# The output's zeroes are sent after W_out's loads instead of among them, and the planner's priorities are set anew

## The chip, the core and the metric

One NeuronCore of a Trainium2 chip runs the whole program. The metric is the device time of one execution in microseconds, median of several runs. Engines are named as the profile names them: PE (TensorE matmul; PEld its weight loads), DVE (VectorE), ACT (ScalarE), POOL (GpSimd), SP (SyncE, which here only issues DMAs).

## What is computed

Three stages follow each other. (1) A Nystrom attention for 4 batches of 8 heads, 576 tokens, 64 wide, with 32 landmarks per head. (2) A mixture of 8 experts, top-1: each token goes to one expert and is multiplied by its gate. (3) A dense MLP with a leaky ReLU whose slope is given per hidden unit.

```python
A = sm(q, k_lm); Bm = sm(q_lm, k_lm); C = sm(q_lm, k)
Z = Bm.T / (norm1(Bm) * norminf(Bm) + 1e-06)
for _ in range(6):
    Z = 2 * Z - Z @ Bm @ Z
x = A @ Z @ C @ v
logits = x @ w_gate
out[i] = gate_w[i] * (relu(x[i] @ w1[e]) @ w2[e])
h = x @ w_in
g = maximum(h, 0) + alpha * minimum(h, 0)
return g @ w_out
```

## The kernel before

Attention is done per batch b and per group g of four heads: `attend_c` makes the landmark-to-token side (C, Bm and Y = C v), `attend_a` the token-to-landmark side (A). `attention_post` iterates Z and makes the routing logits: once for batch 0 alone (stream "post0"), once for the other three (stream "post"). The rest works on one pair of batch and expert at a time. The expert of the first token of batch 0 is read as soon as batch 0's logits are there (`first_expert` writes `e0i`; `weights` reads it on SP and loads that expert's W1 and W2), and this first pair is done in straight code while the other batches are still in attention. The other pairs are in a list, and a hardware loop (`For_i` in `run`) does one per pass; in these inputs there are two passes. One pair is: landmark rows (`landmark_rows`, W1 folded with the attention's small factors into the fp16 pair MW), `moe_h` (hidden tile of the expert, MW times xT), `moe_y` (times W2), transposes, `moe2_h` (times W_in), `moe2_out` (times W_out) and `rows_out`, which scatters the finished rows to the output by an indirect DMA on POOL. Every product is made of three fp16 passes from a high and a low part, so each weight is loaded as float64 words, narrowed to float32 on DVE (three instructions per pair of row blocks, `narrow`), squared and summed on ACT for a scale, and split into two fp16 parts on ACT and DVE (`split`).

W_out's sixteen row blocks come in eight pairs, by way of two stages of SBUF (`st64`, names st_4 to st_11 in the order): the load of a pair waits until the pair two before it has been narrowed. The narrowed pairs lie in room that is free by then (tiles W, MW and xT), and are split to WO at the end. The rows of the output that no pair scatters must be zero: `clear` sends the tile `zero` to the whole output by 18 DMAs of 256 KB, and a scatter may start only when they have landed.

No engine's order is written by hand. Each piece of work is a generator (a stream) that yields one instruction at a time, and `Plan.run` picks, over all streams, which instruction is emitted next: it has a cost for each instruction (`Lane.cost`), takes the stream that could start first, and lets a stream of lower rank go before it if that one could start within `patience + EAGER * (difference of rank)` (`by`). Ranks are numbers in the table `RANKS` (per b and g) and at the streams. `until` holds a stream back in the plan alone; the waits on the chip come from the data. `keep_warm` puts fill matmuls (`fill`, L1728, zero times ones) in front of a PE instruction for which the plan expects PE to wait. The chosen order is fixed when the program is built, each engine runs its own list in order, and SP's list is the order of the DMAs.

Of the kernel before, what the change touches and what calls it, by code (L numbers as in the profile page):

```python
# [18 lines left out]
LM = 32  # L19
TG = 18  # L20
# [184 lines left out]
class Plan:  # L205
# [4 lines left out]
    PHASE = 600  # L210
    EAGER = -62.784

# [172 lines left out]
class Kernel:  # L385
# [41 lines left out]
    def constants(self):  # L427
# [28 lines left out]
        self.have.add("constants")  # L456
        self.streams["constants"].own = -64.376
        def iota(name, n, pattern, base=0, mult=0, parts=P, dt=F32):
# [71 lines left out]
    def loads(self):  # L530

        for b in range(self.B):
            for g in range(2):
                heads = slice(4 * g, 4 * g + 4)
                self.streams["loads"].own = RANKS[b][g] + -54.682
                for nm, src in (("k", self.k), ("q", self.q)):
                    self.raw[nm, b, g] = t = yield Get(self.S["qk"])
                    yield self.dq.dma_start(t, src[b, heads].rearrange("h (p j) d -> (h p) j d", j=TG))
                    self.have.add((nm, b, g))
                if (b, g) == (0, 0):  # L540
                    self.streams["values"] = yield Fork(self.values(), -58.523)

    def values(self):

        for b in range(self.B):
            for g in range(2):
                heads = slice(4 * g, 4 * g + 4)
                if (b, g) != (0, 0):
                    self.streams["values"].own = RANKS[b][g] + -58.501
                self.raw["v", b, g] = t = yield Get(self.S["v"])  # L550
                src = self.v[b, heads]
                yield self.dq.dma_start(t[:, :, :4].rearrange("p h t d -> p h (t d)"), src[:, : 4 * P].rearrange("h (p t) d -> p h (t d)", t=4))
                yield self.dq.dma_start(t[:64, :, 4], src[:, 4 * P :].rearrange("h p d -> p h d"))
                self.have.add(("v", b, g))
                if (b, g) == (0, 0):
                    self.tc.prologue_barrier()

    def sums(self):
# [3 lines left out]
        for b in range(self.B):  # L562
            for g in range(2):
                self.streams["sums"].own = RANKS[b][g] + -55.120
                i = 2 * b + g
# [23 lines left out]
    def turn(self):  # L589
# [8 lines left out]
        for b in range(self.B):  # L598
            for g in range(2):
                self.streams["turn"].own = RANKS[b][g] + -60.592  # L600
                dst = yield Get(self.S["qkT"])
# [70 lines left out]
    def attend_c(self, b, g):  # L672
# [61 lines left out]
    def attend_a(self, b, g):  # L734
# [31 lines left out]
        self.have.add(("P", b, g))  # L766
        self.streams["store", b, g] = yield Fork(self.store(b, g, parts), -53.748)

# [7 lines left out]
    def attention_post(self, bs):  # L776
# [79 lines left out]
        if b == 0:  # L856
            self.streams["post0"].own = -64.244
        big = yield Get(self.big)
# [52 lines left out]
        for n, bb in enumerate(bs):  # L911
# [18 lines left out]
            if bb == 0:  # L930
                yield from self.first_expert(L[0:1, 0, 0, :])
                self.streams["post0"].own = 69.663
            yield Fork(self.used(bb, AT))
        self.have.add(("x", bs[-1]))
        if b:
            yield self.until(("routed", 0))
            self.streams["post"].own = -67.282
        yield from self.route(bs, L)
# [36 lines left out]
    def route(self, bs, L):  # L975
# [82 lines left out]
        if b == 0:  # L1058

            i0 = self.ar.tile([P, 5], F32, tag="r_i0", name="r_i0")  # L1060
            yield dve.scalar_tensor_tensor(i0, code[:, 0], self.e0c, row[:, 0], op0=ALU.is_equal, op1=ALU.mult)
            yield dve.tensor_scalar(self.idx0, i0, float(self.NT), None, op0=ALU.add)
            self.have.add("idx0")
            self.streams["post0"].own = -56.297
        table = self.table[:, b * E : (b + nb) * E].rearrange("p q t -> p (q t)")
# [137 lines left out]
    def landmark_rows(self, MT, slots, late=0.0):  # L1203
# [25 lines left out]
        yield ended(kids)  # L1229
        scale = yield Fork(self.scale_of("w1", 4), -61.376)  # L1230
        yield ended([scale])
# [37 lines left out]
    def early(self):  # L1269
# [11 lines left out]

        self.streams["early_loads"] = yield Fork(loads(), 65.505)
        kids = []
# [41 lines left out]
    def convert(self, name, n, amax=None, low="d", load=None, first=0):  # L1325
# [8 lines left out]
        yield ended(kids)  # L1334
        scale = yield Fork(self.scale_of(name, n // 2, amax), -63.884)
        yield ended([scale])
# [11 lines left out]
    def weight2(self, name, src, amax, low, first=0):  # L1348
# [9 lines left out]
        if name == "wi":  # L1358
            self.streams["wi_loads"] = yield Fork(self.fetch(name, src, range(first, 16, 2), arrived), -71.763)
        else:  # L1360
            self.streams["wo_loads"] = yield Fork(self.fetch(name, src, range(first, 16, 2), arrived), -65.336)
        yield from self.convert(name, 16, amax, low, lambda i: self.narrowed(name, i, arrived), first)
# [191 lines left out]

    def moe2_out(self, ts):

# [51 lines left out]
    def pre(self):  # L1608

        yield self.until(("P", 0, 0), ("P", 0, 1), *([("used", self.n_early - 4)] if self.n_early else ["early"]))  # L1610
        self.streams["first"].own = -64.283
# [4 lines left out]
        self.streams["first"].own = -52.364  # L1616
# [3 lines left out]
        self.streams["first"].own = -61.768  # L1620
        yield from self.moe2_h(True)
        self.have.add("h2")

    def weights(self):
# [3 lines left out]
        yield from self.load_expert(bass.ds(e0, 1), ["w1"])  # L1628
        self.streams["rows"] = yield Fork(self.landmark_rows(self.MT[:, 0:2], [self.big] * 2), -64.966)
        yield self.until("early")  # L1630
        self.streams["weights"].own = -54.431
        yield from self.load_expert(bass.ds(e0, 1), ["w2"])
        self.streams["weights"].own = 64.801
        yield from self.convert("w2", 8, low='d')
# [32 lines left out]
    def clear(self):  # L1667

        yield self.until('y')
        for t in range(self.NT // P):  # L1670
# [48 lines left out]
    def run(self):  # L1719
# [15 lines left out]
        with tc.manual_schedule(engines={ET.PE, ET.DVE, ET.Activation, ET.Pool, ET.SP}):  # L1735
# [24 lines left out]
            for _ in range(10):  # L1760
# [7 lines left out]
                "first": Stream(self.pre(), -58.952),  # L1768
                "weights": Stream(self.weights(), -54.630),
                "rooms": Stream(self.rooms(), -55.921),  # L1770
                "post": Stream(self.attention_post(list(range(1, self.B))), -55.955),
                "early": Stream(self.early(), 70.830),
                "wi": Stream(self.weight_in(), 70.305),
                "wo": Stream(self.weight_out(), 72.429),
                "clear": Stream(self.clear(), 73.613),
                "experts": Stream(self.experts(), 70.932),
                "out": Stream(self.first_out(), -64.384),
                "next": Stream(self.first_next(), -69.294),
                "next_w1": Stream(self.next_w1_late(), -69.303),
                "next_w2": Stream(self.next_w2('d'), -60.504),  # L1780
            }
            for b in range(self.B):
                for g in range(2):
                    self.streams["c", b, g] = Stream(self.attend_c(b, g), RANKS[b][g] + -68.234)
                    self.streams["a", b, g] = Stream(self.attend_a(b, g), RANKS[b][g] + 58.649)
            for lane, ns in ((self.dq, 600), (self.dve, 1200), (self.act, 2000), (self.gp, 1800), (self.pe, 700 + 213 * 10)):
# [40 lines left out]
```

## Time and profile before

| | |
|---|---|
| median of 3 runs | 532.61 us (532.55 to 534.73) |
| the profiled execution | 531.96 us, of which 527.9 us are the span from the first to the last instruction |
| PE busy | 505.1 us, 96% of the span |
| DVE busy | 297.6 us, 56% |
| ACT busy | 260.1 us, 49% |
| POOL busy | 88.2 us, 17% |
| DMA | 64.47 MB, mean 122 GB/s |
| granted TensorE clock | 0.998 |

In time: attention and the first pair's expert run to about 151 us, `moe2_h` of the first pair to 205 us, its `moe2_out` to 257 us, and the two passes of the loop fill the rest. PE's 96% count a matmul from its issue to its modelled end, so a wait of a matmul inside a group can be hidden in it, and the 173 fill matmuls are counted as work too. The figures between the first instruction and 260 us are the ones that the change can move: the loop's code is the same but for a few neighbours exchanged.

### The profile page before, as it was taken

What the parts mean: (1) busy time and instruction counts of PE and PEld (TensorE: products, weight loads), DVE (VectorE), ACT (ScalarE), POOL (GpSimd) and SP (SyncE); (2) the same over time, 40 slices, a digit from 0 to 9 for tenths busy, and PEclk for the clock granted to TensorE, in tenths of its full rate; (3) what the DMA queues carried; (4) which work ended last, traced back from release to release, by engine and by line L of the source; (5) the groups of instructions that cost most, each with busy time, mean ns of one, the idle gap of its engine ahead of it and who ended that gap; (6) DMA issues with size and microseconds to landing.
All of it is one profiled execution on the core that took longest, in us unless ns stands there. A gap on an engine that the chain in (4) does not pass through costs nothing.

```text
span 527.9 us, 12141 instructions
## 1 busy us (share of the span) xinstructions
PE 505.1 (96%) x4808; PEld 333.1 (63%) x4808; DVE 297.6 (56%) x712; ACT 260.1 (49%) x579; POOL 88.2 (17%) x139
## 2 busy tenths in 40 slices
PE   9899988999999699999999999999999999999996
PEld 6777765877477476445655876744475577684444
DVE  6878899869999798306242566820023256584000
ACT  4665646684678469426332458810023245883000
POOL 4888200000114433002100000000010000000101
PEclk9999999999999999999999999999999999999999
DMA  8997548734798722801002390000000229000100
GB/s 298 309 331 259 172 143 271 261 107 137 214 230 240 268 87 84 280 1 60 32 1 50 78 327 7 1 8 33 20 30 0 50 45 339 23 0 0 40 20 31
DMA packets 50682, 64.47 MB, mean 122 GB/s; under 512 B 20320, under 2 KB 34032, under 8 KB 50640
## 3 DMA queue, kind: packets, MB, share of 16 engines
q1 hardware_dynamic: 49536, 60.34, 37.1%
q0 software_dynamic: 1104, 3.54, 1.8%
q8 instruction: 30, 0.49, 0.4%
q14 instruction: 12, 0.10, 0.1%
HBM read 49.50 MB, written 10.62 MB: 114 GB/s over the span
## 4 chain that ended last, share of the span: by engine, by line
PE 74%; DVE 10%; issue 6%; DMA 3%; POOL 2%; ACT 1%; POOLq 0%; SPq 0%; ACTq 0%; DVEq 0%
PE mm L81 70%; PE big L81 2%; DMA out<-st,idxc 2%; PE mm L1728 2%; DVE MW L81 1%; DMA st<-in_moe_w_out 1%; DVE W L81 1%; DVE WIa L81 1%; DVE mm L81 1%; DVE T L81 1%; DVE hgA L81 1%; POOL WIa L81 1%; DVE g L81 1%; POOL hgB L81 1%; DVE mx L81 0%
## 5 line engine op out<-in xcount | busy, mean ns | idle before, releaser
L81 PEld LDWEIGHTS <-hgA 128*128 128x128 f16 (+1 forms) x864 | 70.5, 102 | 69.1 <-issue 5.8
L81 PEld LDWEIGHTS <-WIa 128*128 128x128 f16 x864 | 84.2, 98 | 31.3 <-issue 9.8
L81 PE MATMUL mm<-WO,hgA 128*128 128x512 f16 (+1 forms) x432 | 72.8, 344 | 0.0
L81 PE MATMUL mm<-WO,hgB 128*128 128x512 f16 (+1 forms) x432 | 72.8, 344 | 0.0
L81 PE MATMUL mm<-W,hgA 128*128 128x512 f16 (+1 forms) x432 | 72.7, 344 | 0.1
L81 PE MATMUL mm<-yB,WIa 128*128 128x320 f16 x432 | 61.5, 299 | 4.9 <-DVE g L81 3.7
L81 POOL DMA_INDIRECT out<-st,idxc x12 | 12.3, 1027 | 287.9 <-ACT st L81 282.8
L81 ACT ACTIVATE st<-mm,fac 128x512 f32<-128x512 f32 (+1 forms) x15 | 9.7, 644 | 99.3 <-PE mm L81 99.2
L81 PEld LDWEIGHTS <-hgB 128*128 128x128 f16 (+1 forms) x432 | 35.3, 102 | 36.1 <-issue 3.3
L81 PE MATMUL mm<-yA,WIa 128*128 128x256 f16 x432 | 50.6, 273 | 2.3 <-DVE g L81 1.7
L81 ACT ACTIVATE g<-mm 128x256 f32<-128x256 f32 (+1 forms) x96 | 39.2, 412 | 22.4 <-PE mm L81 13.8
L81 DVE SCALAR_TENSOR_TENSOR mm<-g,oma,mm 128x256 f32<-128x256 f32 (+1 forms) x80 | 41.0, 517 | 9.1 <-ACT g L81 8.5
L81 PE MATMUL mm<-xT,MW 128*128 128x320 f16 (+1 forms) x288 | 36.9, 286 | 2.4 <-ACT st L81 1.8
L81 PEld LDWEIGHTS <-MW 128*128 128x128 f16 x288 | 27.8, 98 | 9.9 <-issue 1.7
L81 PEld LDWEIGHTS <-WIb 128*128 128x128 f16 x288 | 28.2, 99 | 7.3 <-issue 0.4
L81 ACT ACTIVATE junk<-mm 128x512 bf16<-128x512 f32 (+1 forms) x27 | 15.5, 573 | 34.3 <-PE mm L81 34.0
L81 ACT COPY qkT<-mm 128x512 f32<-128x512 f32 (+1 forms) x48 | 22.5, 525 | 18.7 <-PE mm L81 18.7
L81 DVE COPY idxc<-idxn 128x5 int32<-128x5 int32 x2 | 0.3, 173 | 54.9 <-issue 43.9
L81 ACT ACTIVATE hgA<-mm 128x256 f16<-128x256 f32 (+1 forms) x48 | 19.3, 410 | 15.0 <-PE mm L81 14.6
L81 DVE TENSOR_TENSOR hgA<-mm,hgA 128x256 f16<-128x256 f32 (+1 forms) x40 | 18.2, 455 | 14.1 <-ACT hgA L81 13.9
L81 DVE SCALAR_TENSOR_TENSOR hgA<-mm,hgA 128x256 f16<-128x256 f32 (+1 forms) x48 | 20.7, 454 | 9.3 <-ACT hgA L81 9.3
L81 ACT ACTIVATE junk<-W 128x1024 bf16<-128x1024 f32 x21 | 22.2, 1056 | 7.5 <-DMA W<-in_moe_w 7.0
(286 smaller groups left out, 751.2 us busy)
## 6 DMA issues: line engine op xcount, KB each, us to landing
W<-in_moe_w SPq DMA_DIRECT2D x8, 1024.0 KB, 7.9
st<-in_moe_w_out SPq DMA_DIRECT2D x16, 512.0 KB, 5.1
hgA<-in_moe_w_in SPq DMA_DIRECT2D x10, 512.0 KB, 6.5
qk<-in_k SPq DMA_DIRECT2D x8, 576.0 KB, 5.6
qk<-in_q SPq DMA_DIRECT2D x8, 576.0 KB, 7.6
out<-zero SPq DMA_DIRECT2D x18, 256.0 KB, 4.7
v<-in_v SPq DMA_DIRECT2D x8, 512.0 KB, 5.1
W<-in_moe_w SPq DMA_DIRECT2D x8, 512.0 KB, 5.1
```

The source lines that it names most:

```text
L81: r = getattr(self.lane.engine, name)(*a, **k)
L1728: nc.tensor.matmul(o[:, :256], self.ones16, self.zero.bitcast(F16), start=True, stop=True)
```

## The change

`clear` waits in the plan for W_out to be loaded and narrowed too; `first_out` does not wait for `clear` any more, but the first pair's scatters do. All ranks, the table `RANKS` and `EAGER` have new numbers, so the planner's order of everything up to the loop is a new one. One activation of `attend_c` has lost a cost that was set by hand (the plan's own formula stands for it). No instruction of the computation is added or taken away; the plan issues 174 fill matmuls where it issued 173.

```diff
-RANKS = [[-74.375, -56.288], [-49.431, -65.912], [71.374, -74.373], [72.660, -62.802]]
+RANKS = [[-190.251, -162.415], [-189.669, -24.286], [-21.570, 79.087], [95.553, -68.442]]
...
-    EAGER = -62.784
+    EAGER = -23.848
...
-        yield act.activation(EC.rearrange("p (m j w) -> p m j w", m=LM, w=2), turned, AF.Exp, bias=nm2[:, 0:1], scale=0.125 / TG, accum_out=sums[:, 0:1]).takes(1.0)
+        yield act.activation(EC.rearrange("p (m j w) -> p m j w", m=LM, w=2), turned, AF.Exp, bias=nm2[:, 0:1], scale=0.125 / TG, accum_out=sums[:, 0:1])
...
-    def moe2_out(self, ts):
+    def moe2_out(self, ts, first=False):
...
-                    yield Fork(self.rows_out(x, t))
+                    yield Fork(self.rows_out(x, t, first))
...
-    def rows_out(self, ps, t):
+    def rows_out(self, ps, t, first):
...
         yield Put(ps)
+        if first:
+            yield self.until("clear")
         yield self.gp.indirect_dma_start(
...
     def clear(self):
 
-        yield self.until('y')
+        yield self.until("y", ("wo", "float32"))
         for t in range(self.NT // P):
...
     def first_out(self):
 
-        yield self.until("h2", "clear", ("wo", 0))
+        yield self.until("h2", ("wo", 0))
...
-            yield from self.moe2_out(ts)
+            yield from self.moe2_out(ts, True)
...
-                "constants": Stream(self.constants(), 56.007),
-                "post0": Stream(self.attention_post([0]), -64.166),
+                "constants": Stream(self.constants(), -68.342),
+                "post0": Stream(self.attention_post([0]), -168.986),
...
-                "clear": Stream(self.clear(), 73.613),
+                "clear": Stream(self.clear(), -178.670),
```

The first place is SP's list around the second half of W_out's loads (st_8 to st_11 are the pairs that begin with row blocks 8, 10, 12 and 14; x_lst is the list of pairs). Before:

```order
L81 DMA_TRANSPOSE yB<-y_120 128x4x64 x2
L81 DMA out<-zero 512x1x128 x3
L81 DMA st_8_2750<-in_moe_w_out 128x1024 x2
L81 DMA out<-zero 512x1x128 x9
L81 DMA st_9_2868<-in_moe_w_out 128x1024 x2
L81 DMA out<-zero 512x1x128
L1792 TENSOR_LOAD x_lst
L1792 ISA x2
L81 DMA st_10_2965<-in_moe_w_out 128x1024 x2
L81 DMA st_11_3051<-in_moe_w_out 128x1024 x2
L81 TENSOR_LOAD x_lst
```

And now, on SP at the same place:

```order
L81 DMA_TRANSPOSE yB<-y_120 128x4x64 x2
L81 DMA st_8_2745<-in_moe_w_out 128x1024 x2
L81 DMA st_9_2854<-in_moe_w_out 128x1024 x2
L1794 TENSOR_LOAD x_lst
L1794 ISA x2
L81 DMA st_10_2948<-in_moe_w_out 128x1024 x2
L81 DMA st_11_3034<-in_moe_w_out 128x1024 x2
L81 DMA out<-zero 512x1x128 x18
L81 TENSOR_LOAD x_lst
```

The five zeroes further up have left too: all 18 now stand between the last load of W_out and the reading of the list, behind which the next expert's loads come.

The second place is DVE's list from batch 0's logits (L) to the number of its expert (e0i); WIa<-hgA narrows an early part of W_in, T, amx, asum and AT belong to `attend_a` of other groups. Before:

```order
L81 COPY L_1310<-mm_1311 128x40
L81 STREAM_TRANSPOSE AT_1340<-T_6_1147 128x576
L81 TENSOR_REDUCE m_1351<-L_1310 1x1
L81 STREAM_TRANSPOSE T_5_1102<-big_1103 128x576
L81 TENSOR_SCALAR d_1352<-L_1310,m_1351 1x8
L81 TENSOR_REDUCE amx_1366<-T_5_1102 128x18
L81 TENSOR_TENSOR d_1352<-d_1352,dsc 1x8
L81 TENSOR_TENSOR T_5_1102<-T_5_1102,amx_1366 128x576
L81 TENSOR_REDUCE m_1351<-d_1352 1x1
L81 STREAM_TRANSPOSE T_7_1356<-big_1368 128x576
L81 TENSOR_SCALAR e0i<-m_1351 1x1
```

And now, on DVE at the same place:

```order
L81 COPY L_1135<-mm_1136 128x40
L81 TENSOR_SCALAR rs_1128<-sums_1127 128x2
L81 TENSOR_SCALAR Ys_132<-mm_1228,rs_869 128x64
L81 TENSOR_REDUCE m_1265<-L_1135 1x1
L81 RECIPROCAL rs_1128<-rs_1128 128x2
L81 TENSOR_SCALAR d_1266<-L_1135,m_1265 1x8
L81 TENSOR_TENSOR T_5_966<-T_5_966,asum_1032 128x576
L81 TENSOR_TENSOR d_1266<-d_1266,dsc 1x8
L81 SCALAR_TENSOR_TENSOR WIa<-hgA,WIa 128x1024
L81 TENSOR_REDUCE m_1265<-d_1266 1x1
L81 STREAM_TRANSPOSE AT_1288<-T_5_966 128x576
L81 TENSOR_SCALAR e0i<-m_1265 1x1
```

Over DVE's whole list up to e0i, seven instructions that stood ahead of it now stand behind it, and none the other way: two T transposes, one amx, one subtraction T<-T,amx, and of the narrowing of W_in one TENSOR_SCALAR and two SCALAR_TENSOR_TENSOR. Behind "idxc<-idx", some ten instructions after the first expert's W2 scale, the lists of DVE before and now are the same up to the loop but for a few neighbours exchanged.

The third place is PE's list around the landmark rows of the first expert (big<-W,MT; NB is the first product of "post", ss_w the sum of squares for the scale of W1's rows). Before:

```order
L1728 MATMUL mm_1591<-zero,ones_68 128x256
L81 MATMUL mm_1591<-NB_1567,bd 128x384
L81 MATMUL mm_1600<-v_1480,CT_1559 32x64 x20
...
L81 MATMUL big_1587<-W_86,MT 32x512 x8
L81 MATMUL big_1601<-W_86,MT 32x512 x8
```

And now, on PE at the same place:

```order
L81 MATMUL mm_1523<-v_1279,CT_1511 32x64 x20
L81 MATMUL big_1561<-W_86,MT 32x512 x8
...
L1730 MATMUL mm_1598<-zero,ones_68 128x256
L81 MATMUL mm_1598<-NB_1582,bd 128x384
L81 MATMUL big_1562<-W_86,MT 32x512 x8
L1730 LDWEIGHTS ones_68
```

The first half of the rows has moved ahead of NB, with 19 fills between the halves. Counted over PE's list, 71 fills stand ahead of the first half where 98 did, 78 between it and the first product of `moe_h` (xT,MW) where 54 did, and 25 behind where 21 did. From `moe_y` on PE's list is the same as before.

## Rows read from the trace of the kernel before

**Rows 1.** Chain of waits: start us, length us, what; from `moe2_h` to the last pass.
```profile
172.85 6.93 DMA st<-in_moe_w_out
...
193.60 62.81 PE mm L81 x422
...
257.01 32.82 PE mm L81 x229
```
**Rows 2.** Windows: PE, PEld, DVE, ACT, POOL busy, clock, DMA share, GB/s; three stretches.
```profile
170.00:180.00 10.00, 8.30 (x66) 5.96 (x64) 6.38 (x14) 5.69 (x13) 4.66 (x3) 1.00 1.10 357
180.00:194.00 14.00, 11.01 (x88) 8.56 (x88) 12.86 (x22) 8.04 (x21) 3.60 (x3) 1.00 0.32 116
194.00:257.00 63.00, 62.39 (x420) 32.87 (x419) 28.40 (x50) 32.93 (x57) 10.23 (x10) 1.00 0.27 90
```
**Rows 3.** Timeline of DVE, 174 to 184 us; idle before and its releaser in brackets.
```profile
176.01 0.28 DVE L81 TENSOR_SCALAR x_at<-iop,x_rank,x_a 32x32 f16<-32x32 f32 x1
179.88 0.69 DVE L81 TENSOR_SCALAR MW<-st 128x1024 int32<-128x1024 int32 x1 [3.59 <-DMA st<-in_moe_w_out]
```
**Rows 4.** Timeline of PE, 128 to 200 us.
```profile
182.80 1.79 PE L81 MATMUL mm<-yB,WIa 128*128 128x320 f16 x12 [3.70 <-DVE g L81]
```
**Rows 5.** Timeline of SP, 145 to 220 us.
```profile
162.05 1.38 SPq L81 DMA_DIRECT2D st<-in_moe_w_out  x2
163.47 8.42 SPq L81 DMA_DIRECT2D out<-zero  x9
171.99 1.62 SPq L81 DMA_DIRECT2D st<-in_moe_w_out  x2
...
175.26 11.24 SPq L81 DMA_DIRECT2D st<-in_moe_w_out  x4
188.81 0.56 SPq L81 DMA_DIRECT2D mtn<-MT  x1
204.76 8.49 SPq L81 DMA_DIRECT2D W<-in_moe_w  x10
```
**Rows 6.** Timeline of DVE: the last narrowing instruction of pair 6.
```profile
165.76 1.21 DVE L81 SCALAR_TENSOR_TENSOR W<-st,W 128x1024 int32<-128x1024 int32 x1
```
**Rows 7.** Loads of W_out on SP, issue to landing: pairs 10, 12 and 14, in this order.
```profile
DMA to landing us min/median/max: 5.3/6.1/6.9
...
DMA to landing us min/median/max: 6.5/6.9/7.3
...
DMA to landing us min/median/max: 3.3/3.8/4.3
```
**Rows 8.** Timeline of DVE: first instructions on pairs 12 and 14.
```profile
186.06 0.68 DVE L81 TENSOR_SCALAR MW<-st 128x1024 int32<-128x1024 int32 x1
...
190.45 1.01 DVE L81 TENSOR_SCALAR xT<-st 128x1024 int32<-128x1024 int32 x1
```
**Rows 9.** Windows as in rows 2: the first 118 us as one.
```profile
0.00:118.00 118.00, 109.43 (x1906) 84.18 (x1906) 96.40 (x244) 73.43 (x178) 49.11 (x105) 1.00 0.72 240
```
**Rows 10.** Waits of PE, 0 to 116 us: in total, times, longest; the largest two.
```profile
PE big L1728 <- ACT EB L81: 2.6, 1, 2.6
PE mm L81 <- DVE NB L81: 1.5, 1, 1.5
```
**Rows 11.** Timeline of DVE: the expert's number is written.
```profile
73.98 0.10 DVE L81 TENSOR_SCALAR e0i<-m 1x1 int32<-1x1 f32 x1
```
**Rows 12.** Groups of DVE by form: busy, mean ns of one; the kinds that moved.
```profile
L81 DVE SCALAR_TENSOR_TENSOR WIa<-hgA,WIa 128x1024 int32<-128x1024 int32 x10 | 12.5, 1249 | 0.0
L81 DVE TENSOR_TENSOR T<-T,amx 128x576 f32<-128x576 f32 x8 | 7.0, 869 | 0.0
```
**Rows 13.** Timeline of PE, 60 to 131 us.
```profile
86.84 1.95 PE L81 MATMUL big<-W,MT 64*32 64x512 f32 x32
...
89.42 1.59 PE L1728 MATMUL mm<-zero,ones 128*128 128x256 f16 x13
...
97.92 2.13 PE L81 MATMUL mm<-xT,MW 128*128 128x256 f16 x18
```
**Rows 14.** Waits of SP, 0 to 120 us, the largest two.
```profile
SPq L81 <- PE mm L81: 38.0, 13, 13.8
SPq L81 <- POOL parts L81: 18.1, 5, 9.7
```
**Rows 15.** Timeline of PE: landmark rows of the next expert.
```profile
221.13 1.95 PE L81 MATMUL mm<-W,mtn 64*32 64x512 f32 x32
```
**Rows 16.** Timeline of POOL: the first scatter.
```profile
237.15 1.19 POOL L81 DMA_INDIRECT out<-st,idxc  x1 [26.33 <-ACT st L81]
```
**Rows 17.** Windows as in rows 2: one with the least, one with nine zeroes' traffic.
```profile
156.00:160.00 4.00, 3.43 (x33) 2.74 (x31) 4.00 (x9) 3.90 (x9) 1.94 (x1) 1.00 1.35 151
168.00:172.00 4.00, 3.79 (x29) 2.60 (x28) 3.96 (x6) 3.82 (x9) 0.97 (x1) 1.00 1.14 345
```

More of the change, by code (lines that the diff above doesn't have):

```diff
@@ L456, in constants @@
         self.have.add("constants")
-        self.streams["constants"].own = -64.376
+        self.streams["constants"].own = -182.905
         def iota(name, n, pattern, base=0, mult=0, parts=P, dt=F32):
@@ L534, in loads @@
                 heads = slice(4 * g, 4 * g + 4)
-                self.streams["loads"].own = RANKS[b][g] + -54.682
+                self.streams["loads"].own = RANKS[b][g] + -135.434
                 for nm, src in (("k", self.k), ("q", self.q)):
@@ L563, in sums @@
             for g in range(2):
-                self.streams["sums"].own = RANKS[b][g] + -55.120
+                self.streams["sums"].own = RANKS[b][g] + -193.537
                 i = 2 * b + g
@@ L766, in attend_a @@
         self.have.add(("P", b, g))
-        self.streams["store", b, g] = yield Fork(self.store(b, g, parts), -53.748)
+        self.streams["store", b, g] = yield Fork(self.store(b, g, parts), -169.245)
     def store(self, b, g, parts):
@@ L856, in attention_post @@
         if b == 0:
-            self.streams["post0"].own = -64.244
+            self.streams["post0"].own = -65.619
         big = yield Get(self.big)
@@ L936, in attention_post @@
             yield self.until(("routed", 0))
-            self.streams["post"].own = -67.282
+            self.streams["post"].own = -137.701
         yield from self.route(bs, L)
@@ L1280, in loads @@
                 self.have.add(("loaded", i))
-        self.streams["early_loads"] = yield Fork(loads(), 65.505)
+        self.streams["early_loads"] = yield Fork(loads(), 95.023)
         kids = []
@@ L1334, in convert @@
         yield ended(kids)
-        scale = yield Fork(self.scale_of(name, n // 2, amax), -63.884)
+        scale = yield Fork(self.scale_of(name, n // 2, amax), -176.626)
         yield ended([scale])
@@ L1358, in weight2 @@
         if name == "wi":
-            self.streams["wi_loads"] = yield Fork(self.fetch(name, src, range(first, 16, 2), arrived), -71.763)
+            self.streams["wi_loads"] = yield Fork(self.fetch(name, src, range(first, 16, 2), arrived), -164.840)
         else:
-            self.streams["wo_loads"] = yield Fork(self.fetch(name, src, range(first, 16, 2), arrived), -65.336)
+            self.streams["wo_loads"] = yield Fork(self.fetch(name, src, range(first, 16, 2), arrived), -192.828)
         yield from self.convert(name, 16, amax, low, lambda i: self.narrowed(name, i, arrived), first)
@@ L1610, in pre @@
         yield self.until(("P", 0, 0), ("P", 0, 1), *([("used", self.n_early - 4)] if self.n_early else ["early"]))
-        self.streams["first"].own = -64.283
+        self.streams["first"].own = -176.600
         yield from self.moe_h(True)
@@ L1615, in pre @@
         yield self.dve.tensor_copy(self.idxc, self.idx0)
-        self.streams["first"].own = -52.364
+        self.streams["first"].own = -137.454
         yield from self.moe_y((0, 1, 2, 3, 4), self.gate[:, 0], True)
@@ L1619, in pre @@
         yield self.until("rooms")
-        self.streams["first"].own = -61.768
+        self.streams["first"].own = -135.600
         yield from self.moe2_h(True)
@@ L1765, in run @@
                 "sums": Stream(self.sums(), 2),
-                "constants": Stream(self.constants(), 56.007),
-                "post0": Stream(self.attention_post([0]), -64.166),
[L1768 to L1774, printed above, removed]
-                "clear": Stream(self.clear(), 73.613),
[L1776 to L1780, printed above, removed]
+                "constants": Stream(self.constants(), -68.342),
+                "post0": Stream(self.attention_post([0]), -168.986),
+                "first": Stream(self.pre(), -79.218),
+                "weights": Stream(self.weights(), 79.632),
+                "rooms": Stream(self.rooms(), -66.559),
+                "post": Stream(self.attention_post(list(range(1, self.B))), -164.819),
+                "early": Stream(self.early(), 71.164),
+                "wi": Stream(self.weight_in(), -75.754),
+                "wo": Stream(self.weight_out(), -66.781),
+                "clear": Stream(self.clear(), -178.670),
+                "experts": Stream(self.experts(), -70.639),
+                "out": Stream(self.first_out(), -183.331),
+                "next": Stream(self.first_next(), -135.603),
+                "next_w1": Stream(self.next_w1_late(), -193.387),
+                "next_w2": Stream(self.next_w2('d'), -168.460),
             }
```

22 lines of the change are left out of this document (11 added, 11 removed).

## The prediction

> **What bounds the kernel now.** I read the chain of waits first, then busy time by windows, then the timelines of the engines in the stretch where the chain leaves PE. The chain says where time can be won at all: from 193.6 us to the end it is PE matmul after PE matmul, in long unbroken pieces, so nothing that another engine does there shortens the program [rows 1]. The two passes of the loop and the first pair's last two products can only start earlier. What can be won lies ahead of 193.6 us. There the windows show a stretch that is neither PE's nor DVE's: between 170 and 180 us DVE is busy 6.38 of 10 us and PE 8.30, while the DMA engines are full at 357 GB/s; behind 194 us PE is busy 62.39 of 63 us [rows 2]. The timelines name the cause. DVE ends its work at 176.3 us and stands for 3.59 us, because the pair of W_out that it is to narrow next has not landed [rows 3]. The PSUM tiles that DVE should empty stay full, and PE stands 3.70 us until a result of DVE that is queued behind that narrowing [rows 4]. The same DMA is in the chain [rows 1].
>
> Why is it late? It is pair 10. Its stage is free when pair 6 has been narrowed, at 165.76 + 1.21 = 166.97 us [rows 6]. SP issues its load only at 171.99 us, because nine zeroes stand ahead of it in SP's list and take from 163.47 to 171.89 us to issue [rows 5]; and it needs 5.3 to 6.9 us to land, where pair 14, which goes alone, needs 3.3 to 4.3 us [rows 7].
>
> **Term one, the zeroes out of W_out's way.** With no zero ahead, SP issues pair 10 at about 167 us. At the same 6.9 us of landing, the slower of its two loads, it is there by 167.0 + 1.4 + 6.9 = 175.3 us (1.4 us for two issues, as at pair 8 [rows 5]), ahead of the 176.3 us at which DVE asks for it. The wait of 3.59 us goes, and what was queued behind it on DVE, ACT and PE moves up by it: **-3.6 us**. It cannot be much more, since PE's own wait is 3.70 us. Pair 12 is not what is late next: SP issues it at 175.26 us, when pair 8 is narrowed, and even at its 7.3 us of landing it comes at about 183 us, where DVE, 3.6 us earlier, wants it at 182.5 us (186.06 before [rows 8]); part of that 7.3 us was the crowd that is now gone. Pair 14 is what is next: it is issued behind the narrowing of pair 10, and before the change DVE began it at 190.45 us [rows 8], just when its last load, issued at about 186.1 us, had taken its 4.3 us [rows 7]. Both ends move together, so there is no new wait as long as it lands as quickly. But now 18 zeroes follow right behind it. The bounds are 4.3 us as now (nothing) and 6.9 us as under zeroes (2.6 us); zeroes that come behind should matter less than zeroes ahead, so I take **+0.4 us**.
>
> **Term two, the zeroes at their new place.** They begin when pair 14 has been issued, now at 186.5 - 3.6 = 182.9 us. 18 times 0.262 MB are 4.72 MB; at 345 GB/s, the rate under nine zeroes [rows 17], that is 13.7 us, so they have landed at about 200 us. Behind them in SP's list stand the reading of the list and the next expert's loads. Those begin at 204.76 us before [rows 5], held by W_out's splits, which free W1; shifted they want to begin at 201 us. The scatter that now waits for the zeroes stands on POOL at 237.15 us [rows 16], more than 30 us later, and only scatters are behind it there. Both are hidden by the 15.7 us of W_out matmuls in between: **0 us**. If the zeroes went at 151 GB/s, the least of a window in which they moved [rows 17], it would be 31 us; that is a rival below.
>
> A rule of the Trainium skill bears on this place (DMA: Bandwidth & Descriptors, "Queues, rings and completion order"): SP owns one row of rings, and each DMA engine takes descriptors from its ring in order. By it the next expert's loads could not pass the zeroes, as W_out's pair 10 did not pass them before; the trace agrees [rows 5, 7]. The sum stays as it is unless the zeroes drain slowly.
>
> **Term three, the new order of attention.** It can go either way. For a gain: seven DVE instructions no longer stand ahead of e0i. Two of them take 1.249 us each and one 0.869 [rows 12]; the other four are shorter, 0.71 to 0.77 each in the same view. That makes 6.4 us, so the first expert's number, written at 73.98 us [rows 11], and with it its W1, should come up to 6 us earlier. Against it: PE has to issue the same matmuls and one fill more before `moe_y`, in order. It was busy 109.43 of the first 118 us [rows 9], so 8.6 us of waiting is all that can go, 0.8 us of it at the very start; the two large late ones, 2.6 us for EB and 1.5 us for NB [rows 10], are 4.1 us. What moved behind e0i is not saved either: DVE must do it beside `moe_h`, where some 4.6 us more of it now stands (the same T, amx and AT instructions), and PE may wait there instead. The bounds are -4.1 us (both waits gone, none new) and +4.6 us (all of the delayed DVE work met by PE). I take **-1.5 us**, a little over a third of the two waits: nearer to the gain, because half of the landmark rows need not wait for NB any more, yet 78 fills instead of 54 stand between them and `moe_h`, and PE issues these whether or not it has to wait.
>
> **The loop** keeps its PE list; in DVE's and ACT's lists a few neighbours change: 0.
>
> **Sum.** -3.6 + 0.4 + 0 - 1.5 = -4.7 us. The profiled execution (531.96 us, the span of 527.9 and 4.1 around it) becomes 527.3. The median of the runs is 0.65 above it, so in its terms I forecast **527.9 us**.
>
> **Rivals.**
> *The new order gives the gain back (no change).* Term one holds, but DVE's delayed work makes PE wait in `moe_h`: with +2 us instead of -1.5 the sum is -1.2, or 531.4 us. For it: DVE was busy 96.40 of 118 us and is nearly the second bound there [rows 9]. Against it: it must eat all that e0i wins.
>
> *W1 is held up on SP (slower).* The second load of W1 now stands behind a load of v, and the second half of W1 behind a store of parts. SP has waited up to 13.8 us for a PE product that frees v and up to 9.7 us for POOL to make parts [rows 14]. If the store holds SP for 9.7 us, the second half of the landmark rows is that much late. PE comes to them 27 fills earlier, and thirteen took 1.59 us [rows 13], so it has some 3.3 us more to lose: it waits 6.4 us, and 532.6 - 3.2 + 6.4 = 535.8 us. It decides from a hold of about 9 us. Against it: the AT from which those parts are made stands right ahead of e0i on DVE, so the store is ready soon after.
>
> *The next expert is late (slower).* This is the case of the ring order above. At 151 GB/s the zeroes land at 182.9 + 31 = 214 us, 13 us after the loads want to go. The rows that need W1 stood at 221.13 us [rows 15], and its last load, issued by 213.3 us [rows 5], had at 4.3 us of landing [rows 7] some 3.6 us to spare. PE would wait 9 us: 532.6 - 4.7 + 9 = 536.9 us. The slow window held transposes by DMA too, and few zeroes, so I hold it unlikely.
>
> *Both terms in full.* -3.7 - 4.1 and, of PE's other waits before 118 us (8.6 - 0.8 - 4.1 = 3.7 us), half: 532.6 - 9.7 = 522.9 us.
>
> **Numbers.** A measurement of this kernel can tell about 0.5%, 2.7 us, from no change. Chances: the forecast's case, 524.5 to 529.9 us, 0.58; both in full 0.10; gain given back 0.22; W1 held up 0.07; the next expert late 0.03. Faster by over 0.5% is 0.58 + 0.10 = 0.68, within it 0.22, slower 0.10. The range goes from 522.9 (both in full) to 532.2 us, which takes in the case where the gain is given back and leaves out about 0.1 above and less below.
>
> **What would show it.** Right: no wait of DVE for W_out near 176 us; PE's wait of 3.7 us gone; the 18 zeroes on SP from about 180 us and landed by 200; PE unbroken from about 189 us on; the first xT,MW of `moe_h` 0 to 4 us before 97.9 us [rows 13]. Wrong: a new DVE wait at pair 14, PE waits in `moe_h` of more than 3 us, W1's landmark rows later than 86.8 us [rows 13], or a wait of PE for W at the next expert's rows.

## The result, and the profile after

The changed kernel takes **523.66 us** (median of 4 runs, 523.16 to 524.16) where the kernel before took 532.58 us in the same comparison: a ratio of 0.984 (95% interval 0.981 to 0.988), 8.9 us less. The forecast was 527.9 us with a range of 522.9 to 532.2: the side was right and the range holds the time, but the gain is nearly twice the one that was summed up.

| | before | after |
|---|---|---|
| profiled execution, its span | 531.96, 527.9 us | 524.16, 519.9 us |
| first moe_y matmul (W,hgA) | 118.56 us | 112.94 us |
| first matmul of the loop | 257.01 us | 248.13 us |
| last scatter issued | 523.90 us | 515.07 us |

The loop's first matmul is 8.88 us earlier and the last scatter 8.83: the loop itself is unchanged. (The spans differ by 8.0 only, since the profile after ends 4.9 us after its last scatter begins and the one before 4.0.) Of the 8.88 us, **5.62** are there when `moe_y` begins and **3.26** come between there and the loop. The two profiled executions differ by 7.8 us, less than the medians: the one before has a mean granted clock of 0.998, while in its runs beside the experiments the kernel before had 0.985 to 0.999, with a median of 0.992 to 0.993, and the changed kernel had 0.997 to 1.000 in all of its runs.

First the windows, with the columns of [rows 2]: the first line is the kernel before up to its `moe_y`, the others are the kernel after; they answer to [rows 2, 9].

```profile
0.00:118.56 118.56, 109.99 (x1954) 84.68 (x1955) 96.92 (x245) 73.90 (x179) 49.11 (x105) 1.00 0.71 239
```

```profile
0.00:112.94 112.94, 108.45 (x1955) 83.60 (x1956) 97.91 (x245) 73.22 (x179) 49.98 (x105) 1.00 0.74 251
...
170.00:180.00 10.00, 9.41 (x79) 7.34 (x78) 9.87 (x18) 6.06 (x16) 1.86 (x3) 1.00 0.51 172
180.00:194.00 14.00, 13.96 (x115) 10.96 (x113) 11.89 (x24) 9.63 (x25) 6.06 (x6) 1.00 1.06 315
```

The hole of 170 to 180 us is filled: DVE is busy 9.87 of 10 us instead of 6.38, PE 9.41 instead of 8.30, and the full load of the DMA engines now lies in 180 to 194 us, where PE does not notice it (13.96 of 14 us). Ahead of `moe_y` the first two lines say that PE stood 4.49 us (112.94 - 108.45), where before it stood 8.57 (118.56 - 109.99).

SP's timeline after shows why, for the first of these. It answers to [rows 5]; the pairs 8, 10, 12 and 14 are the four single rows, then the zeroes.

```profile
153.91 1.00 SPq L81 DMA_DIRECT2D st<-in_moe_w_out  x2
161.39 0.81 SPq L81 DMA_DIRECT2D st<-in_moe_w_out  x2
169.65 0.81 SPq L81 DMA_DIRECT2D st<-in_moe_w_out  x2
176.70 0.80 SPq L81 DMA_DIRECT2D st<-in_moe_w_out  x2
177.55 16.78 SPq L81 DMA_DIRECT2D out<-zero  x18
197.78 0.55 SPq L81 DMA_DIRECT2D mtn<-MT  x1
198.63 6.56 SPq L81 DMA_DIRECT2D W<-in_moe_w  x10
```

Pair 10 leaves at 161.39 us, 10.6 us earlier than before. DVE and PE at this place, after ([rows 3, 4, 8, 15, 16] before):

```profile
170.61 0.67 DVE L81 TENSOR_SCALAR MW<-st 128x1024 int32<-128x1024 int32 x1
182.16 1.06 DVE L81 TENSOR_SCALAR xT<-st 128x1024 int32<-128x1024 int32 x1 [0.78 <-DMA st<-in_moe_w_out]
```

```profile
174.08 1.79 PE L81 MATMUL mm<-yB,WIa 128*128 128x320 f16 x12 [0.59 <-DVE g L81]
212.25 1.95 PE L81 MATMUL mm<-W,mtn 64*32 64x512 f32 x32
```

```profile
228.27 1.19 POOL L81 DMA_INDIRECT out<-st,idxc  x1 [26.33 <-ACT st L81]
```

DVE takes pair 10 (first row) without a wait; its only wait for W_out is 0.78 us at pair 14. PE's wait of 3.70 us has become 0.59, for a result of DVE that still stands behind its narrowing of pair 10. The next expert's rows and the first scatter stand exactly 8.88 us earlier, as all of PE's list there does, and the scatter still waits for ACT and not for the zeroes.

For the first stretch, the waits of PE ahead of 116 us. [rows 10] has the two largest before, for EB and NB, together 4.1 us; the others before are these:

```profile
PE big L1728 <- DVE T L81: 1.3, 1, 1.3
PE big L81 <- issue: 0.9, 1, 0.9
PE mm L1761 <- PEq L1812: 0.8, 1, 0.8
PE mm L81 <- POOL WIa L81: 0.6, 1, 0.6
PE mm L81 <- DVE RW L81: 0.5, 1, 0.5
```

That makes 8.2 us. All of them after:

```profile
PE big L81 <- DVE nm L81: 1.1, 1, 1.1
PE big L1730 <- DVE MW L81: 0.9, 1, 0.9
PE mm L1763 <- PEq L1814: 0.8, 1, 0.8
PE mm L81 <- DVE WIa L81: 0.8, 1, 0.8
PE big L1730 <- ACT EB L81: 0.5, 1, 0.5
PE mm L81 <- ACT qkT L81: 0.3, 1, 0.3
```

They are 4.4 us. EB has 0.5 us left of 2.6, NB nothing of 1.5: that is 3.6 of the 3.8 us. The others are not the same ones, but make 3.9 us where they made 4.1; one for MW (0.9 us) is new, in `moe_h`. And the number of the first expert is there at 64.52 us instead of 73.98 [rows 11]:

```profile
59.97 0.19 DVE L81 COPY L<-mm 128x40 f32<-128x40 f32 x1
...
64.52 0.10 DVE L81 TENSOR_SCALAR e0i<-m 1x1 int32<-1x1 f32 x1
```

### The profile page after: what moved, and what is told of

Same layout as the page of the kernel before. It is cut to its first block, busy times and chain, and to the rows that moved or that the text cites. A ratio compares the mean times of both kernels' runs of the same rounds, so it can differ in the third digit from the quotient of the medians.

```text
span 519.9 us, 12146 instructions
## 1 busy us (share of the span) xinstructions
PE 503.6 (97%) x4809; PEld 332.0 (64%) x4809; DVE 299.4 (58%) x712; ACT 259.4 (50%) x579; POOL 88.8 (17%) x139
## 4 chain that ended last, share of the span: by engine, by line
PE 79%; DVE 9%; issue 6%; DMA 4%; ACT 1%; POOL 0%; POOLq 0%; SPq 0%; ACTq 0%; DVEq 0%
PE mm L81 73%; PE big L81 4%; PE mm L1730 2%; DVE WIa L81 2%; DMA out<-st,idxc 2%; DVE W L81 1%; DVE MW L81 1%; DMA st<-in_moe_w_out 1%; DVE mm L81 1%; DVE hgA L81 1%; DMA qk<-in_k 1%; DVE g L81 1%; ACT st L81 0%; PE big L1730 0%; ACT MW L81 0%
```

## Experiments

### The two parts apart: e1, e2

e1 is the kernel before with the edits on the zeroes (and `first`, handed down to `rows_out`) and none on ranks; only SP's list differs from that of before.

```diff
-        yield self.until('y')
+        yield self.until("y", ("wo", "float32"))
...
-        yield self.until("h2", "clear", ("wo", 0))
+        yield self.until("h2", ("wo", 0))
...
         yield Put(ps)
+        if first:
+            yield self.until("clear")
```

> The kernel before with the move of the zeroes alone; its ranks stay. Theory (the two parts of the change add up, each in its own stretch): DVE's wait of 3.59 us for pair 10 and PE's of 3.70 us go, nothing ahead of 150 us moves; 532.6 - 3.3 = 529.3 us. Rival (the zeroes' gain comes only because the new order gives W_out's loads more room): PE still waits 2 us or more near 176 us, 531 us or more.

e2 is the changed kernel with these edits undone and the old rank of `clear` (73.613), so that the zeroes stand among W_out's loads again; the other engines' lists are those of the changed kernel.

> The changed kernel with the zeroes back among W_out's loads, at the places where the kernel before has them; the lists of the other engines are those of the changed kernel. Theory (the parts add up): moe_y starts 5.6 us earlier than before, the wait for pair 10 is there again with 3.6 us; 532.6 - 5.6 = 527.0 us. Rival (the W_out stretch is set by the DMA engines and not by the work ahead of it): moe_y is earlier by 5.6 us but the wait for W_out grows by the same, 530 us or more.

Measured: e1 528.7 us, ratio 0.992 (0.989 to 0.995); e2 527.45 us, ratio 0.990 (0.985 to 0.995). In the traces the two stretches come out like this (us; the first column is jitter and order together, since the first microseconds of single runs differ by some 0.5):

| | moe_y begins | from there to the loop |
|---|---|---|
| before | 118.56 | 138.45 |
| e1, zeroes moved | 118.07 | 135.45 |
| e2, new ranks | 113.76 | 139.35 |
| after | 112.94 | 135.19 |

So each part works in its own stretch. The wait for pair 10 is there in e2 (DVE, then PE):

```profile
174.57 0.69 DVE L81 TENSOR_SCALAR MW<-st 128x1024 int32<-128x1024 int32 x1 [3.06 <-DMA st<-in_moe_w_out]
```

```profile
177.49 2.45 PE L81 MATMUL mm<-yB,WIa 128*128 128x320 f16 x12 [3.19 <-DVE g L81]
```

and gone in e1, where DVE's only wait for W_out is at pair 14, with 0.78 us as in the changed kernel:

```profile
179.19 1.79 PE L81 MATMUL mm<-yB,WIa 128*128 128x320 f16 x12 [0.58 <-DVE g L81]
```

The zeroes' move is worth 3.0 us in these profiles in the old order and 4.2 in the new one. The rivals (a gain that needs the new order; a W_out stretch that takes back what attention gains) both fall: the wait for W_out in e2 is shorter than before, not longer (3.06 us for 3.59). e2's stretch is 0.9 us longer than that of before all the same, and that goes with the granted clock. At PE's wait it fell to the lower of its two levels (1.2 of 2.4 GHz): it is 0.95 in 180 to 200 us, and the twelve matmuls behind the wait took 2.45 us instead of 1.79. So it is in five of the six profiled executions that have the zeroes among W_out's loads (e2, e4, e5, e6, e11, after waits of 2.98 to 3.75 us; clock 0.83 to 0.95 in 180 to 200 us); only that of before kept 1.00. The longest of them is e4:

```profile
183.33 3.36 PE L81 MATMUL mm<-yB,WIa 128*128 128x320 f16 x12 [3.72 <-DVE g L81]
```

From `moe_y` to the loop these five take 138.70 to 140.69 us. The seven with the zeroes behind the loads or left out (after, e1, e3, e7 to e10) have a clock of 1.00 there and take 134.86 to 135.45. (e12 has another plan and waits of its own.) So the wait costs up to 2.2 us more than the profile of before shows, and the move saves that too; this is the likely reason why the medians differ by more than the two profiled executions.

### The zeroes' price at the new place: e3

The loop over the 18 DMAs of `clear` runs over none.

```diff
-        for t in range(self.NT // P):
+        for t in range(0):
```

> The changed kernel without the 18 zeroes: rows of the output that no pair scatters are left unwritten; nothing else changes in any list. Theory (behind W_out's last load they are hidden but for pair 14): DVE's wait of 0.78 us for pair 14 goes and with it at most 0.8 us: 523 us. Rival (zeroes cost nothing there, pair 14 is late by its own issue): no change, 523.7 us. Second rival (the zeroes also hold the next expert's loads and the first scatter): 521 us or less.

Measured: 523.0 us, ratio 0.981 (0.978 to 0.985), against 0.984 for the changed kernel. DVE's wait at pair 14 is gone, and the DMA engines are nearly idle where the zeroes went:

```profile
180.00:194.00 14.00, 14.00 (x116) 11.05 (x115) 12.28 (x25) 9.78 (x25) 6.51 (x6) 1.00 0.08 28
```

But from `moe_y` to the loop it takes 135.06 us (113.25 to 248.31): 0.13 us less than with the zeroes, in one profile of each. The 0.78 us were nearly hidden. SP begins the next expert's ten loads at 196.05 us without the zeroes and at 198.63 with them, and PE does not wait for them either way. The zeroes are as good as free there.

### What held the old order: e4, e5, e6

e4 gives SP the first expert's number as a constant (it is 0 for these inputs).

```diff
-        e0 = yield self.dq_value(self.e0i[0:1, 0:1], self.E - 1)
+        op = self.dq_value(self.e0i[0:1, 0:1], self.E - 1)
+        op.issue = lambda: 0
+        e0 = yield op
```

> The kernel before, with the number of the first expert given as a constant where SP loads its W1 and W2 (the computation of the number stays, only SP does not wait for it); every list but SP's is unchanged. Theory (W1's arrival sets the start of moe_h): W1's loads start some 7 us earlier, the landmark rows and moe_h move up by 5 us or more, 527 us. Rival (in the order before, DVE's unbroken work from 69 to 85 us holds PE at NB, which stands ahead of the landmark rows): the rows stay at 86.8 us, moe_h within 0.5 us of 97.9 us, 532.5 us.

It told nothing: 533.25 us, ratio 1.001 (0.998 to 1.004), because W1's loads did not move (76.32 us). A load of v stands ahead of them on SP and waited until 75.9 us for PE to free v. e5 moves that load behind W1 (LATE_V is (3, 1), the last batch and group; its file is a line longer, so line 81 reads L82):

```diff
+                    if (b, g) == LATE_V:
+                        op.issue = lambda o=op.issue: self.late.append(o)
...
+            if i == 7:
+                op.issue = lambda o=op.issue: [o(), *[x() for x in self.late]][0]
```

> The kernel before as in e4 (the first expert's number is a constant for SP), and the last load of v, which kept W1 waiting on SP in e4, is moved behind W1's eight loads. W1's loads can go as soon as SP is there, near 66 us instead of 76. Theory (DVE's unbroken work from 69 to 85 us holds NB, and the rows stand behind NB on PE): the landmark rows stay within 0.7 us of 86.8 us and the first xT,MW of moe_h within 0.7 us of 97.9 us; 532.6 us. Rival (W1's arrival alone set them): rows 4 us or more earlier, 528.5 us or less.

Measured: 531.66 us, ratio 1.001 (0.998 to 1.004). W1 now goes 11.5 us earlier, and nothing follows. SP, then PE:

```profile
64.44 5.98 SPq L82 DMA_DIRECT2D W<-in_moe_w  x8
```

```profile
85.90 1.95 PE L82 MATMUL big<-W,MT 64*32 64x512 f32 x32
...
96.98 2.13 PE L82 MATMUL mm<-xT,MW 128*128 128x256 f16 x18
```

The first product on NB, which stands ahead of the rows, in the kernel before and in e5:

```profile
84.95 0.91 PE L81 MATMUL mm<-NB,bd 128*128 128x384 f32 x2 [1.49 <-DVE NB L81]
```

```profile
84.01 0.91 PE L82 MATMUL mm<-NB,bd 128*128 128x384 f32 x2
```

Rows and `moe_h` are 0.94 us earlier, and so is everything since the first 20 us of this run (L at 68.13 instead of 69.06 us), so behind that W1's early arrival gained 0.0 us. In the old order the rows stood behind NB on PE, and W1 merely came in time: its last load had landed at 86.60 us, and the second half of the rows began at 87.72. (In e5 PE does not wait for NB, although NB is no later: the granted clock is 0.92 in 80 to 100 us, and the matmuls ahead of NB took longer by what PE had waited.) e6 then takes work from DVE, the engine that was busy without a break at this place:

```diff
-N1 = dict(early="ddddd", wi="dddddddd", wo="dddddddd")
+N1 = dict(early="dddDD", wi="dddddddd", wo="dddddddd")
...
+            if by == 'D':
+                op.issue = lambda: None
```

> e5 with DVE relieved: of the narrowing of W_in's last two early pairs the two later instructions each are left out, four of 1.2 us (at 80.30, 85.48, 94.71 and 101.30 us before); W_in's values there are then wrong. Theory (DVE is what binds once W1 is early): NB and the rows come 1.2 us earlier by the first, moe_h another 1.2 us by the third and 1.2 us by the second or less; the first xT,MW near 95 us, 529.5 to 530.5 us. Rival (it is PE's own list that binds there): under 1 us, 532 us.

Measured: 532.26 us, ratio 1.001 (0.996 to 1.005). The landmark rows are at 85.50 us and the first xT,MW at 96.58, 0.3 us earlier than in e5 once the runs' common shift of 0.13 is taken off; `moe_y` begins 0.8 us earlier by the same reckoning (116.67 against 117.63). So 4.9 us less work on DVE bring 0.8, where the theory expected 2.4 or more and the rival, PE's own list, under 1. But this does not decide between them. NB was ready on DVE at 82.6 us, which is the theory's 1.2 us earlier than in e5, and PE came to it only at 83.72: the clock, 0.93 in 80 to 100 us, had drawn out PE's list ahead of it by as much as PE waited there before. What less work on DVE is worth at the full clock stays open. Shown is that W1's late arrival alone did not hold the old order.

### W1 in the new order: e7

```diff
-        yield from self.load_expert(bass.ds(e0, 1), ["w1"])
+        for op in self.load_expert(bass.ds(e0, 1), ["w1"]):
+            op.issue = lambda o=op.issue: (o(), o())[1]
+            yield op
```

> The changed kernel with each of the eight loads of the first expert's W1 sent twice, so 2.1 MB more, some 6 us at 350 GB/s, ahead of the landmark rows. Theory (in the new order W1's arrival has no slack left, e0i's 9.5 us went into it): the second half of the rows comes 5 us or more later, moe_y by 4 to 6 us; 528 to 530 us. Rival (DVE's work binds, W1 has slack): moe_y later by under 2 us, 525.5 us at most.

Measured: 549.31 us, ratio 1.032 (1.026 to 1.038). The delay is not the 6 us of the bytes: the second sending of each load waited for the first, and W1 was complete some 27 us later. So the edit asks a coarser question than was meant. PE's waits for W1 in it:

```profile
PE big L81 <- DMA W<-in_moe_w: 12.1, 6, 3.2
```

The last landmark rows end at 108.99 us instead of 81.96, the first xT,MW comes at 118.45 instead of 90.95 (27.5 later), and the program ends 25.7 us later. Nearly all of W1's delay arrives at the end, as any delay far above the slack would; how large the slack is, e7 cannot tell. (The granted clock is 0.65 in 80 to 100 us, where PE waits, so a little of the 27 us is slower matmuls.) The trace of the changed kernel tells it: W1's last load had landed at 79.57 us, and the second half of the rows begins at 80.87, behind NB. So W1 has some 1.3 us of slack there, about as much as in the kernel before (1.1 us), and no wait of PE listed for the changed kernel is for W1.

### The fills: e8 to e11

In e8 and e10 every second fill of the changed kernel is left out, in e11 of the kernel before; e9 is the changed kernel again, on the chip of e10 to e12.

```diff
             for i in range(n):
-                self.fill(self.tiles[name])
+                if i % 2 == 0:
+                    self.fill(self.tiles[name])
```

> The changed kernel with every second fill matmul left out; the plan and all other lists stay. Theory (the fills stand where PE would wait, so they are waiting that is counted as work): moe_y starts within 0.7 us of 112.9 us, PE's idle time ahead of it grows by some 8 us, 523.7 us within 1. Rival (the fills themselves hold PE's list, since the plan put more of them than there is waiting): moe_y 1.5 us or more earlier, 522 us or less. Second rival (with fewer fills the granted clock falls): slower, with a clock under 0.95 in some stretch ahead of 113 us.

> The changed kernel unaltered, to stand on the same chip as the next three. Every theory: ratio to the kernel before 0.984, as it was, within 0.004.

> The kernel of e8 beside the changed kernel. Theory (some of the fills hold PE's list; e8's profile has the loop's start 1.98 us earlier): 2 us under e9, ratio 0.980. Rival (that was the scatter of single runs): within 0.8 us of e9.

> The kernel before with every second fill left out. Theory (in the old order PE's list ahead of moe_h holds more than it waits, which is why e5 and e6 gained so little): moe_y 2 us or more earlier than 118.6 us, ratio 0.996 or less. Rival (DVE's work is what holds the old order): moe_y earlier by under 1 us and PE's waits longer by what the fills took, ratio 0.998 to 1.000.

Measured: e8 523.21 us, ratio 0.984 (0.978 to 0.990); e9 523.26 us, 0.985 (0.982 to 0.987); e10 524.88 us, 0.985 (0.982 to 0.987); e11 535.57 us, 1.007 (1.005 to 1.009). So half the fills change nothing in the new order that the runs can tell (e10's median is 1.6 us above e9's, not 2 us under it, and the runs of both spread from 522.4 to 525.8) and cost 0.7% in the old one, where neither theory nor rival had expected a loss.

The profile of e8 alone would mislead: its loop begins 1.98 us earlier than in the changed kernel, e10's 1.36 earlier than e9's, so the fills do hold PE a little. With fewer of them it shows what PE meets between W1's rows and `moe_h` in the new order. Among e8's waits, and not in the changed kernel, are these:

```profile
PE mm L81 <- DVE RW L81: 0.8, 2, 0.4
...
PE mm L81 <- ACT junk L81: 0.8, 1, 0.8
...
PE mm L81 <- DVE sc_w1c L81: 0.5, 1, 0.5
...
PE mm L81 <- DVE NB L81: 0.4, 1, 0.4
```

They are small ones for results of DVE and ACT, and none is for W1. In e11, the old order, it is otherwise: the landmark rows begin 1.85 us earlier than before, but take 3.29 us instead of 1.95, since their last part begins only when W1's last load has landed, at 87.19 us:

```profile
84.99 3.29 PE L81 MATMUL big<-W,MT 64*32 64x512 f32 x32
```

The granted clock is not 1.00 everywhere with half the fills (windows as above, where it is the third figure from the end):

```profile
60.00:80.00 20.00, 18.78 (x301) 14.24 (x293) 16.40 (x59) 12.36 (x31) 1.29 (x1) 0.91 0.77 234
```

```profile
80.00:100.00 20.00, 17.25 (x297) 10.33 (x296) 17.19 (x50) 10.89 (x26) 2.10 (x2) 0.94 0.78 244
```

The first is e10, the second e11. The profile of the changed kernel has 1.00 in the first stretch, but so has e8 with half the fills; the profile of before has 1.00 in the second, but e5 and e6 have 0.92 and 0.93 there with every fill. So that the missing fills lowered the clock is not shown. What e10 has won when its loop begins is given back in the second pass of the loop, whose first matmul waits 2.84 us for nothing that the trace shows, and 1.18 us for ACT in the changed kernel (first e10, then after):

```profile
382.27 3.00 PE L81 MATMUL mm<-xT,MW 128*128 128x256 f16 x26 [2.84 <-issue]
```

```profile
381.74 3.44 PE L81 MATMUL mm<-xT,MW 128*128 128x256 f16 x30 [1.18 <-ACT st L81]
```

From the first matmul of the loop to this one it takes 135.26 us in e10 and 133.61 in e9. Another 1.8 us between these two profiled executions lie outside the span (5.9 us in e10, 4.1 in e9), which the trace does not cover.

### One try to go further: e12

The narrowing of W_in's last early pair is held in the plan until MW is split, with half the fills.

```diff
-            yield self.until(("loaded", i))
+            yield self.until(("loaded", i), *([("w1", 1)] if i == 8 else []))
...
-        yield self.until("early")
+        yield self.until(("used", 6))
```

> The changed kernel with half the fills, and with the narrowing of W_in's last early pair held in the plan until W1 has been split to MW (W2's load no longer waits for it in the plan). Theory (two narrowings of 1.13 us stand between W1's scale and MW on DVE, in the chain at 85.57 and 87.42 us): MW and moe_h 1 to 2 us earlier than in e10, the end 0.5 to 2 us earlier. Rival (the narrowing is missing behind, where it holds W2's split or the stages of W_in): the same as e10 or up to 2 us slower.

Measured: 530.11 us, ratio 0.996 (0.994 to 0.998), 5 to 6 us worse than e10. The planner's lists changed with it. `moe_h` begins no earlier (90.34 against 90.31 us), `moe_y` begins 2.6 us later, and new waits follow, the first with a granted clock of 0.91 in 160 to 180 us:

```profile
170.46 4.83 PE L81 MATMUL mm<-yB,WIa 128*128 128x320 f16 x24 [2.57 <-DVE hgA L81]
...
202.51 11.81 PE L81 MATMUL mm<-WO,hgA 128*128 128x512 f16 x54 [1.23 <-DVE hgB L81]
```

The rival's side is right, its "up to 2 us slower" too small: work that is put off is missing behind. No version run here beats the changed kernel.

## Why the prediction was right, and where it fell short

**Term one, -3.6 + 0.4: right.** Measured -3.26 us from `moe_y` to the loop. Each step can be read off: pair 10 was to leave when pair 6 is narrowed (166.97 us, less the 5.6 won ahead: 161.4) and left at 161.39; it landed ahead of DVE; PE's wait went from 3.70 to 0.59 us. Two sizes were off and nearly cancelled: of the 3.6 us some 3.4 arrive at PE (e3, 138.45 to 135.06), which still waits 0.59 us for DVE's own work; and pair 14's wait, put at 0.4 us, is 0.78 on DVE but 0.13 us at the end, by e3. A new wait of DVE at pair 14 stood among the signs of being wrong; it came, and was too short to matter. The 6.9 us of landing were far on the safe side: without the crowd of zeroes pair 10 lands in 4.2 us (median). Not foreseen at all was the clock: the term was read from a profile in which the clock stayed at 1.00 behind the wait, and in five others it fell there.

**Term two, zeroes at the new place, 0 us: right.** They went from 177.55 us, 16.78 us of issuing, at 313 GB/s in the window from 178 to 194 us, near the 345 taken and far from the bound of 151. The next expert's loads began 2.6 us later than without them (e3), inside the slack.

The rule of the Trainium skill cited with this term (DMA: Bandwidth & Descriptors, "Queues, rings and completion order"), by which each DMA engine takes descriptors from its ring in order, is not tested here. Before, pair 10 did land behind the last zero ahead of it (177.3 and 179.8 us against 175.7), but SP also issued them in that order. After, the last zero, issued at 193.46 us, had landed 3.6 us later, before SP issued the first of the next expert's loads at 198.63.

**Term three, the order of attention, -1.5 us: the step that failed, by its size.** It measured -5.62 us (e9: -5.37), outside the bound of -4.1. `moe_h` itself came 6.97 us earlier (90.95 for 97.92), not "0 to 4", and 1.35 of that was lost again ahead of `moe_y`. Three things were missed. First, of the two large waits 3.6 us went and not "a little over a third": PE's idle time ahead of `moe_y` fell by 4.08 us (8.57 to 4.49), just inside the bound. Second, what lies outside it is busy time. The prediction held that 8.6 us of waiting "is all that can go"; but PE's busy time ahead of `moe_y` fell by 1.54 us too (109.99 to 108.45), with one fill more. Counted by themselves the fills took 24.76 us in 30 runs before and 23.26 in 23 runs after:

```profile
0.00:118.56 118.56, 24.76 (x164) 1.00 0.71 239
```

```profile
0.00:112.94 112.94, 23.26 (x165) 1.00 0.74 251
```

I had taken the fills as a fixed cost, "whether or not it has to wait". Third, the number of the expert came 9.46 us earlier, not "up to 6": the logits L are there 9.09 us earlier, since PE's list has their products earlier. I had counted the seven DVE instructions and not what PE did ahead of L. On the other side, the price that I feared, DVE's delayed work met in `moe_h`, was one wait of 0.9 us.

What the runs show of the cause: the gain lies ahead of `moe_y` and comes with the ranks (e2). In the old order two chains came to the landmark rows within about 1 us of each other: NB, for which PE waited 1.49 us, and W1, whose last load landed 1.1 us before the second half of the rows began. An earlier W1 alone therefore gains nothing (e5), and a PE that comes earlier meets W1 (e11). In the new order both have moved, NB on DVE by 5.3 us and W1's last load by 7.0, and W1 is again in time by 1.3 us. What holds PE there is its own list and, with fewer fills, small waits for DVE and ACT (e8). That the landmark rows' half ahead of NB, the early logits and the spread of DVE's work brought this together is argued from the lists and not shown by a run. Which of the rank changes is worth what stays open; a rank moved alone gives another plan, and e12 shows how far that can go wrong.

**The rivals.** "The gain given back by attention" did not occur. "W1 held up on SP" needed a hold of 9 us; the store of parts held it some 1 us. "The next expert late" fell with the zeroes' rate. "Both terms in full" (522.9 us) was nearly what came, at a chance of 0.10; part by part too (3.7 and 5.95 us there, 3.26 and 5.62 measured), only that the rest beyond the two waits came from busy time and not from PE's other waits. The forecast's own case, 524.5 to 529.9 us at 0.58, does not hold the time. With term three outside its bound, the range holds it by its lower end alone, to which half of PE's other waits had been added.

## What to carry to other kernels

A DMA that nobody waits for is not free where it stands in a queue: list what is issued behind it, and move it behind the last load that something waits for, with its own reader's slack checked. For a new order of work, bound the gain by the whole idle time of the engine that binds, and take filler work as waiting too. Do not look for one cause of a stall where two chains come in at the same time: here W1 alone, made early, gave nothing. And look at the granted clock behind each long wait, in more than one execution, before you compare landmarks of two traces.

## What the runs showed of the hardware

With every second fill left out, some 155 instructions of PE fewer (matmuls and weight loads), the second pass of the loop began after 1.84 to 2.84 us of PE standing with no releaser in all four such kernels (e8, e10, e11, e12), and after 1.18 to 1.26 us, for ACT, in all ten with every fill (before, after, e1 to e7, e9). In e10 the DMA table of 370 to 384 us, which spans that gap, has a row that the same table of the changed kernel lacks:

```profile
q8 instruction: 2, 0.03, 0.9%
```

The other three have it too around their gaps. So instructions were being loaded there. The Trainium skill (Runtime: NRT & Kernel Launch, "Instruction fetch mechanics") says that a taken branch to a target outside the fetched window forces a fetch before execution goes on. The trace agrees in kind; that the shorter code moved the loop's start to such a place is argued and was not tried.
